# The range check's verdict spread over the last chunk, and the last output tile in two halves

## The chip, the cores and the metric

One core of a Trainium2 chip runs the whole kernel. The metric is the device time of one execution in microseconds, as the median of several runs. Times inside the kernel come from one profiled execution.

## The reference

Attention with a decay bias, then a feed-forward block. For each of 8 batches and 8 heads (576 positions, 64 wide):

```python
cum = np.cumsum(np.maximum(s, 0.0), axis=-1)
bias = -(cum[:, :, :, None] - cum[:, :, None, :])
scores = np.where(causal, -1000000000.0, scale * q @ k.T + np.minimum(bias, 0.0))
attn = softmax(scores)
x = (attn @ v)                      # to [4608 tokens, 512]
xn = x / sqrt(mean(x * x) + 1e-6) * rms_g
out = (silu(xn @ w_gate) * (xn @ w_val)) @ w_out
```

The weights are 512x1536 and 1536x512, the output is 4608x512 in float32.

## The kernel before, in words

The 4608 tokens are worked in 9 chunks of 512 (c = 0 to 8). `ffn(c)` (L658) is the backbone. It has two parts. First come 12 turns (fb = 0 to 11, counted from 0), each with four matmuls for the gate (L668, into a buffer Gp), a tanh on ACT into T (L671), four matmuls for the value (L677, into Vp), and on DVE the product U from T and Gp (L680) and then Ht from U and Vp (L673, the last one L685). I call the products of turn n Un and Hn. Then comes the output projection: four tiles of 128 tokens (tb = 0 to 3), each of 12 matmuls of 512 columns (L690), an eviction on ACT into `osb` (L695) and a store from the SP queue (L697).

All of Gp, Vp and the accumulators Op of the output tiles come from one pool of four PSUM buffers (`psF`, L101). Each allocation takes the buffer of the fourth one before it, so Gp of turn n+2 waits until Un has been computed, and Vp of turn n+2 until Hn has.

The order of instructions on each engine is written out by the program, since the schedule is manual (L771). Between the groups of matmuls `ffn` calls `step()` (L599), which counts a slot and places the work of the attention for later chunks, and one function from each of several side queues if the queue's condition holds: `run_side(dve_side)` (L630) is the one that matters here. In the last two chunks there is no attention work left. Each engine works through its instructions in order.

The fast path holds only while the values stay in a range. For that the kernel collects the largest magnitudes of k and q in `acc` and the sums of squares in `ss_all`, and `decay_range` (L722) adds sums of the decay. `verdict()` (L741) turns these into one flag: four DVE instructions over the statistics ("the sums", L742 to L747, into `stat`), a transpose of `stat` on TensorE (L750), a maximum over it (L752, `mx`), a transpose of `mx` (L754), and a few one-element instructions on DVE with one Exp on ACT (L756 to L768) that end in `flag_i`. It is called once, after `ffn` of chunk 7 and before that of chunk 8 (L912). At the end every engine loads `flag_i` (L927) and branches (L928): in range it skips `general`, which would compute everything again. On SP the load of the flag stands ahead of the last chunk's stores.

Of the kernel before, what the change touches and what calls it, by code (L numbers as in the profile page):

```python
# [12 lines left out]
AF = mybir.ActivationFunctionType  # L13
ALU = mybir.AluOpType
AX = mybir.AxisListType
# [4 lines left out]
DROP_MAX = 576.0 * 2.0 ** -24  # L20
RANGE_MAX = 75.0
SS_MAX = 1.0e37
# [4 lines left out]
def kernel(  # L27
# [12 lines left out]
    nc = tc.nc  # L40
    B, H, S, D = q.shape
    DM = H * D
# [58 lines left out]
    def psF():  # L101
        return pp.tile([128, DM], FP32, name="psF", tag="F", bufs=4)
# [16 lines left out]
    def psT32():  # L119
        return pp.tile([128, 512], FP32, name="psT32", tag="T", bufs=1)  # L120
# [478 lines left out]
    def step(bare=False):  # L599

        slot[0] += 1
        while pending:
            pending.pop(0)()
        moved = False
        if scaled[0] < len(x_list):
            b, qb = x_list[scaled[0]]
            if ready(3, "AV", b, qb, 1):
                x_scale(b, qb)
                scaled[0] += 1
                if not by_pe(b, qb):  # L610
                    assert xt_seq[0] == (b, qb)
                    xt_dma(*xt_seq.pop(0))
                    done["XT", b, qb] = slot[0] + 4
                    moved = True
        run_side(act_side)
        if not moved and x_seq and slot[0] - last["X"] >= 2:
            b, w, c = x_seq[0]
            if (ready(2, "cast", b, 1) and ready(1, "S", b - 2, 4, 0)
                    and (w == 1 or ready(7, "K", b, c))):
                x_seq.pop(0)  # L620
                kq_dma(b, w, c)
                done["X", b, w, c] = last["X"] = slot[0]
                if b >= KB and (w, c) == (0, NSC - 1) and b + 2 < B:
                    casts(b + 2)
        bare = bare or chunk[0] == 0 and 30 <= phase() <= 33
        if slot[0] % 2 and not bare:
            run_side(v_side)
        if not bare:
            run_side(pool_side)
        run_side(dve_side)  # L630
        if can_s():
            pending.append(do_s(s_seq.pop(0)))
            if t_seq and t_seq[0][0] == 1 and can_t():
                do_t(t_seq.pop(0))
            return
        n = 0
        if can_xt():
            do_xt(xt_seq.pop(0))
            n += 1
        if can_av():  # L640
            do_av(av_seq.pop(0))
            n += 1
        if n < 2 and t_seq and can_t():
            do_t(t_seq.pop(0))
# [13 lines left out]
    def ffn(c):  # L658

        x0 = (c * DM) % RING  # L660
        first[0], chunk[0] = slot[0], c
        Ht = mp.tile([128, FB, DM], BF16, name="Ht", tag="Ht", bufs=2)
        pend = None
        for fb in range(FB):
            fs = slice(fb * 128, (fb + 1) * 128)
            Gp = psF()
            for cc in range(CC):
                nc.tensor.matmul(Gp, lhsT=wg_sb[:, cc, fs], rhs=xnT[:, cc, x0:x0 + DM],  # L668
                                 start=(cc == 0), stop=(cc == CC - 1))
            T = mp.tile([128, DM], FP32, name="T", tag="T", bufs=2)  # L670
            nc.scalar.activation(out=T, in_=Gp, func=AF.Tanh, scale=0.5)  # L671
            if pend is not None:
                nc.vector.tensor_tensor(out=Ht[:, fb - 1, :], in0=pend[0], in1=pend[1], op=ALU.mult)  # L673
            step()
            Vp = psF()
            for cc in range(CC):
                nc.tensor.matmul(Vp, lhsT=wv_sb[:, cc, fs], rhs=xnT[:, cc, x0:x0 + DM],  # L677
                                 start=(cc == 0), stop=(cc == CC - 1))
            U = mp.tile([128, DM], BF16, name="U", tag="U", bufs=2)
            nc.vector.scalar_tensor_tensor(out=U, in0=T, scalar=1.0, in1=Gp,  # L680
                                           op0=ALU.add, op1=ALU.mult)
            pend = (U, Vp)
            if fb < FB - 1:
                step()
        nc.vector.tensor_tensor(out=Ht[:, FB - 1, :], in0=pend[0], in1=pend[1], op=ALU.mult)  # L685
        step()
        for tb in range(4):
            Op = psF()
            for fb in range(FB):
                nc.tensor.matmul(Op, lhsT=Ht[:, fb, tb * 128:(tb + 1) * 128],  # L690
                                 rhs=wout_sb[:, fb, :], start=(fb == 0), stop=(fb == FB - 1))
                if fb % 4 == 3 and fb < FB - 1:
                    step()
            osb = mp.tile([128, DM], FP32, name="osb", tag="osb", bufs=3)
            nc.scalar.activation(out=osb, in_=Op, func=AF.Copy, scale=0.5)  # L695
            r0 = c * DM + tb * 128
            nc.sync.dma_start(out=out[r0:r0 + 128, :], in_=osb)  # L697
            step()

    def load_w(src, dst, i):  # L700
# [21 lines left out]
    def decay_range():  # L722

        def row(i):
            e = 255 + 128 * i
            nc.vector.tensor_scalar(out=rng[:, 4 + i:5 + i], in0=cum[:, e:e + 1], scalar1=-1.0,
                                    scalar2=None, op0=ALU.mult)
            nc.scalar.activation(out=s_sb[:, 0:128 * (i + 1)], in_=cum[:, 0:128 * (i + 1)],
                                 func=AF.Exp, bias=rng[:, 4 + i:5 + i],
                                 accum_out=rng[:, 8 + i:9 + i])  # L730

        def over():
            nc.vector.tensor_copy(out=stat[0:BH, 1:2], in_=rng[:, 0:1])
            nc.vector.tensor_tensor(out=rng[:, 11:12], in0=rng[:, 8:9], in1=rng[:, 9:10],
                                    op=ALU.max)
            nc.vector.tensor_tensor(out=stat[0:BH, 2:3], in0=rng[:, 11:12], in1=rng[:, 10:11],
                                    op=ALU.max)
        dve_side.extend((lambda: chunk[0] == B - 1 and slot[0] % 2, f) for f in [
            lambda i=i: row(i) for i in range(3)] + [over])

    def verdict():  # L741
        nc.vector.tensor_reduce(out=stat[:, 0:1], in_=acc, axis=AX.X, op=ALU.max)  # L742
        okc = mp.tile([128, B * NSC], FP32, name="okc")
        nc.vector.tensor_scalar(out=okc, in0=ss_all, scalar1=SS_MAX, scalar2=None, op0=ALU.is_le)
        low = mp.tile([128, 1], FP32, name="low")
        nc.vector.tensor_reduce(out=low, in_=okc, axis=AX.X, op=ALU.min)
        nc.vector.tensor_scalar(out=stat[:, 3:4], in0=low, scalar1=-1.0, scalar2=1.0,  # L747
                                op0=ALU.mult, op1=ALU.add)
        ps = psT32()
        nc.tensor.matmul(ps[0:4, 0:128], lhsT=stat, rhs=ident_f, is_transpose=True)  # L750
        mx = mp.tile([4, 1], FP32, name="mx")
        nc.vector.tensor_reduce(out=mx, in_=ps[0:4, 0:128], axis=AX.X, op=ALU.max)  # L752
        ps2 = psT32()
        nc.tensor.matmul(ps2[0:1, 0:4], lhsT=mx, rhs=ident_f[0:4, 0:4], is_transpose=True)  # L754
        g = mp.tile([1, 8], FP32, name="g")
        nc.vector.tensor_copy(out=g[:, 0:4], in_=ps2[0:1, 0:4])  # L756

        nc.vector.tensor_scalar(out=g[:, 4:5], in0=g[:, 0:1], scalar1=g[:, 0:1], scalar2=8.0625,
                                op0=ALU.mult, op1=ALU.mult)
        nc.scalar.activation(out=g[:, 5:6], in_=g[:, 4:5], func=AF.Exp, scale=2.0)  # L760
        nc.vector.tensor_scalar(out=g[:, 5:6], in0=g[:, 5:6], scalar1=g[:, 2:3], scalar2=DROP_MAX,
                                op0=ALU.mult, op1=ALU.is_le)
        nc.vector.tensor_scalar(out=g[:, 6:7], in0=g[:, 4:5], scalar1=g[:, 1:2],
                                scalar2=RANGE_MAX, op0=ALU.add, op1=ALU.is_le)
        nc.vector.tensor_scalar(out=g[:, 7:8], in0=g[:, 3:4], scalar1=0.5, scalar2=None,
                                op0=ALU.is_le)
        nc.vector.tensor_tensor(out=g[:, 5:6], in0=g[:, 5:6], in1=g[:, 6:7], op=ALU.mult)
        nc.vector.tensor_tensor(out=flag_i, in0=g[:, 5:6], in1=g[:, 7:8], op=ALU.mult)  # L768


    with tc.manual_schedule():  # L771

# [134 lines left out]
        for c in range(NCH):  # L907
            need(c)
            if c == B - 1:
                decay_range()  # L910
            ffn(c)
            if c == B - 1:  # L912
                verdict()
    fast.close()

    general(ctx, tc, q, k, v, out, wg_sb, wv_sb, wout_sb, g_row, cum, ident_bf, flag_i)
# [182 lines left out]
```

## Time and profile before

| | us |
|---|---|
| median of 3 runs (lowest to highest) | 375.38 (375.37 to 375.68) |
| the profiled execution, its own time | 374.85 |
| its span, first to last instruction | 373.2 |
| start of chunk 7, first gate matmul | 304.07 |
| output projection of chunk 7 | 324.79 to 335.31 |
| start of chunk 8, first gate matmul | 336.01 |
| output projection of chunk 8 | 356.73 to 367.25 |
| last eviction | 367.34 to 367.94 |

A line of the timeline shows the start and duration in us, engine, line of the kernel, operation, output and inputs with their shapes, a count where several are merged, and in brackets the idle time of the engine before it and what ended that. PE is TensorE's matmuls, PEld its weight loads. A matmul's duration includes its passage through the array, so the step from one to the next is shorter than its duration. A line of a stretch shows its bounds and length, for each engine the busy time with the number of instructions, then the granted TensorE clock, the share of the DMA engines and GB/s.

### The profile page before, as it was taken

Reading aid. Unit: us, or ns where it says so; the run is one execution under the profiler, and the core shown is the slowest. Engines: PE = TensorE matmul, PEld = TensorE weight load, DVE = VectorE, ACT = ScalarE, POOL = GpSimd, SP = SyncE. Lnnn points to the kernel's source line nnn. Section 1 sums busy time; section 2 is a strip of 40 time slices with the busy share of each in tenths; the row PEclk is TensorE's granted clock in tenths of the full one; section 3 lists DMA queues with packets and bytes.
Section 4 is the critical chain, followed back from the end, with each engine's and each line's share of the span. In section 5 each row is a group of like instructions: output and inputs, shape, how many; then the busy total and the mean of one; then the engine's idle time right before and its main releaser. Section 6 shows DMA issues by size and latency. Waiting matters only on the chain. (4 is left out here: it accounts for less than half of the span.)

```text
span 373.2 us, 6936 instructions
## 1 busy us (share of the span) xinstructions
PE 347.1 (93%) x2356; PEld 161.4 (43%) x2356; DVE 279.6 (75%) x525; ACT 240.0 (64%) x626; POOL 175.2 (47%) x277
## 2 busy tenths in 40 slices
PE   1777899899999999899999999999999999999993
PEld 1443444454444444444444444444444444444441
DVE  6778988589887878788889897795488548837730
ACT  3787787547877597776778776777677644323321
POOL 5866734974846565779856825523322310000000
PEclk9879999999999999999999999999999999999998
DMA  7999999799997599959999997973310230020012
GB/s 228 192 206 262 148 208 210 122 201 222 127 204 104 52 200 161 159 56 204 147 166 223 139 118 151 122 56 44 99 23 14 44 105 3 0 84 31 0 42 78
DMA packets 125626, 46.22 MB, mean 124 GB/s; under 512 B 104912, under 2 KB 120784, under 8 KB 125584
## 3 DMA queue, kind: packets, MB, share of 16 engines
q0 software_dynamic: 59920, 11.80, 43.9%
q1 hardware_dynamic: 53040, 24.33, 34.7%
q10 hardware_dynamic: 12624, 9.59, 10.2%
q8 instruction: 20, 0.33, 0.4%
q14 instruction: 22, 0.18, 0.2%
HBM read 38.16 MB, written 9.44 MB: 128 GB/s over the span
## 5 line engine op out<-in xcount | busy, mean ns | idle before, releaser
L274 ACT ACTIVATE E<-psS,biasK 128x256 bf16<-128x256 f32 (+3 forms) x352 | 115.1, 416 | 19.7 <-PE psS L250 18.0
L668 PE MATMUL psF<-xnT,wg_sb 128*128 128x512 bf16 x432 | 111.1, 379 | 1.9 <-DMA xnT<-xs_sb 0.8
L677 PE MATMUL psF<-xnT,wv_sb 128*128 128x512 bf16 x432 | 111.1, 379 | 0.1
L690 PE MATMUL psF<-wout_sb,Ht 128*128 128x512 bf16 x432 | 102.3, 379 | 0.0
L283 POOL TENSOR_SCALAR_AFFINE_SELECT E<-E 128x512 bf16<-128x512 bf16 x72 | 51.9, 721 | 92.8 <-ACT E L274 92.0
L671 ACT ACTIVATE T<-psF 128x512 f32<-128x512 f32 x108 | 64.4, 598 | 41.5 <-PE psF L668 38.3
L680 DVE SCALAR_TENSOR_TENSOR U<-T,psF 128x512 bf16<-128x512 f32 x108 | 73.6, 682 | 21.8 <-ACT T L671 21.8
L673 DVE TENSOR_TENSOR Ht<-U,psF 128x512 bf16<-128x512 bf16 x99 | 67.7, 684 | 7.5 <-PE psS L250 0.5
L668 PEld LDWEIGHTS <-wg_sb 128*128 128x128 bf16 x432 | 38.7, 98 | 46.3 <-issue 7.5
L677 PEld LDWEIGHTS <-wv_sb 128*128 128x128 bf16 x432 | 38.6, 98 | 42.8 <-issue 4.6
L690 PEld LDWEIGHTS <-Ht 128*128 128x128 bf16 x432 | 38.7, 98 | 42.0 <-issue 2.3
L338 DVE SCALAR_TENSOR_TENSOR xs_sb<-x_sb,al_all,g_row 128x512 bf16<-128x512 bf16 (+1 forms) x40 | 32.4, 810 | 16.6 <-POOL al_all L331 15.0
L695 ACT ACTIVATE osb<-psF 128x512 f32<-128x512 f32 x36 | 21.4, 595 | 33.7 <-PE psF L690 29.3
L321 ACT ACTIVATE xs_sb<-x_sb 128x512 bf16<-128x512 bf16 (+1 forms) x36 | 22.9, 640 | 21.3 <-DVE x_sb L315 21.2
L175 POOL DMA_DIRECT2D v_sb<-in_v_dram x40 | 35.3, 883 | 0.4 <-issue 0.3
L375 DVE TENSOR_TENSOR acc<-acc,mag 128x1280 bf16<-128x1280 bf16 x32 | 29.5, 936 | 0.4
L250 PE MATMUL psS<-kqT 64*128 64x256 bf16 (+2 forms) x304 | 26.6, 260 | 1.4 <-ACT E L274 1.2
L306 PEld LDWEIGHTS <-E 128*128 128x128 bf16 x320 | 22.5, 99 | 12.1 <-POOL E L283 2.2
L328 POOL TENSOR_SCALAR al_all<-ss_all 128x1 f32<-128x1 f32 (+1 forms) x40 | 11.3, 282 | 27.6 <-ACT xs_sb L321 21.5
L300 PEld LDWEIGHTS <-E 128*128 128x128 bf16 x256 | 20.7, 99 | 8.0 <-DVE x_sb L315 0.8
L331 POOL TENSOR_TENSOR al_all<-al_all,mhalf 128x1 f32<-128x1 f32 (+1 forms) x40 | 22.6, 565 | 3.3
L250 PEld LDWEIGHTS <-kqT 64*128 64x128 bf16 x320 | 10.5, 96 | 29.9 <-issue 28.5
(94 smaller groups left out, 279.7 us busy)
## 6 DMA issues: line engine op xcount, KB each, us to landing
out_dram<-osb SPq DMA_DIRECT2D x36, 256.0 KB, 2.3
kq<-in_q_dram ACTq DMA_DIRECT2D x6, 1024.0 KB, 9.5
v_sb<-in_v_dram POOLq DMA_DIRECT2D x32, 128.0 KB, 7.2
kq<-in_k_dram ACTq DMA_DIRECT2D x2, 1024.0 KB, 10.6
kqn<-in_k_dram POOLq DMA_DIRECT2D x16, 128.0 KB, 4.9
wg_sb<-in_moe_w_gate_dram POOLq DMA_DIRECT2D x2, 768.0 KB, 7.3
wv_sb<-in_moe_w_val_dram POOLq DMA_DIRECT2D x2, 768.0 KB, 10.1
wout_sb<-in_moe_w_out_dram POOLq DMA_DIRECT2D x1, 1536.0 KB, 14.1
```

Of the source, the lines that this page charges most:

```text
L175: nc.gpsimd.dma_start(out=v_sb[0:n, b % 2, c, :, 0:64], in_=v[b, :, c * 128:c * 128 + n, :].rearrange("h p d -> p h d"))
L250: nc.tensor.matmul(pair[par][:, j * W:j * W + M], lhsT=kT, rhs=qT, start=(j == 0), stop=(j == nj - 1))
L274: nc.scalar.activation(out=eo, in_=ei, func=AF.Exp, scale=0.125, bias=biasK[:, kb, bh:bh + 1])
L283: nc.gpsimd.affine_select(out=Ev[:, :, 0:nq], in_=Ev[:, :, 0:nq], pattern=[[0, nh], [1, nq]], compare_op=ALU.is_ge, fill=0.0, base=0, chan ...
L338: nc.vector.scalar_tensor_tensor(out=xs_sb[0:n, (b * NSC + qb) % NX, :], in0=x_sb[0:n, (b * NSC + qb) % NX, :], scalar=al_all[0:n, col:col ...
L375: nc.vector.tensor_tensor(out=acc[:, sl], in0=acc[:, sl], in1=mag[:, sl], op=ALU.max)
L668: nc.tensor.matmul(Gp, lhsT=wg_sb[:, cc, fs], rhs=xnT[:, cc, x0:x0 + DM], start=(cc == 0), stop=(cc == CC - 1))
L671: nc.scalar.activation(out=T, in_=Gp, func=AF.Tanh, scale=0.5)
L673: nc.vector.tensor_tensor(out=Ht[:, fb - 1, :], in0=pend[0], in1=pend[1], op=ALU.mult)
L677: nc.tensor.matmul(Vp, lhsT=wv_sb[:, cc, fs], rhs=xnT[:, cc, x0:x0 + DM], start=(cc == 0), stop=(cc == CC - 1))
L680: nc.vector.scalar_tensor_tensor(out=U, in0=T, scalar=1.0, in1=Gp, op0=ALU.add, op1=ALU.mult)
L690: nc.tensor.matmul(Op, lhsT=Ht[:, fb, tb * 128:(tb + 1) * 128], rhs=wout_sb[:, fb, :], start=(fb == 0), stop=(fb == FB - 1))
```

## The change

Two edits. `verdict()` computes nothing itself any more: it makes its tiles and returns four functions, `sums`, `turn`, `row` and `flag`, with the same instructions as before. For chunk 8 (c == B) they are put on the queue `dve_side` before `ffn(8)`, each with the condition that the slot number is a multiple of 3; so `step()` places one in every third slot, one and a half turns apart. By the order of instructions in the changed kernel, the sums stand on DVE between H0 and U1, the maximum of the transposed `stat` between U2 and H2, the copy of the row between H3 and U4, and the flag between U5 and H5. On TensorE the transpose of `stat` stands between the value matmuls of turn 2 and the gate matmuls of turn 3, the transpose of `mx` between the gate and the value matmuls of turn 4; the Exp stands on ACT between the tanh of turns 5 and 6.

The last output tile (chunk 8, tb = 3) is computed in two halves of 256 columns, each with an accumulator of its own, 12 matmuls, an eviction and a store.

```diff
         for tb in range(4):
-            Op = psF()
-            for fb in range(FB):
-                nc.tensor.matmul(Op, lhsT=Ht[:, fb, tb * 128:(tb + 1) * 128],
-                                 rhs=wout_sb[:, fb, :], start=(fb == 0), stop=(fb == FB - 1))
-                if fb % 4 == 3 and fb < FB - 1:
-                    step()
             osb = mp.tile([128, DM], FP32, name="osb", tag="osb", bufs=3)
-            nc.scalar.activation(out=osb, in_=Op, func=AF.Copy, scale=0.5)
             r0 = c * DM + tb * 128
-            nc.sync.dma_start(out=out[r0:r0 + 128, :], in_=osb)
+            halves = 2 if (c, tb) == (NCH - 1, 3) else 1
+            for i in range(halves):
+                Op = psF()
+                cs = slice(i * DM // halves, (i + 1) * DM // halves)
+                for fb in range(FB):
+                    nc.tensor.matmul(Op[:, cs], lhsT=Ht[:, fb, tb * 128:(tb + 1) * 128],
+                                     rhs=wout_sb[:, fb, cs], start=(fb == 0), stop=(fb == FB - 1))
+                    if fb % 4 == 3 and fb < FB - 1:
+                        step()
+                nc.scalar.activation(out=osb[:, cs], in_=Op[:, cs], func=AF.Copy, scale=0.5)
+                nc.sync.dma_start(out=out[r0:r0 + 128, cs], in_=osb[:, cs])
             step()
...
     def verdict():
...
+        def sums():
+            nc.vector.tensor_reduce(out=stat[:, 0:1], in_=acc, axis=AX.X, op=ALU.max)
+            nc.vector.tensor_scalar(out=okc, in0=ss_all, scalar1=SS_MAX, scalar2=None, op0=ALU.is_le)
+            nc.vector.tensor_reduce(out=low, in_=okc, axis=AX.X, op=ALU.min)
+            nc.vector.tensor_scalar(out=stat[:, 3:4], in0=low, scalar1=-1.0, scalar2=1.0,
+                                    op0=ALU.mult, op1=ALU.add)
+
+        def turn():
+            ps = psT32()
+            nc.tensor.matmul(ps[0:4, 0:128], lhsT=stat, rhs=ident_f, is_transpose=True)
+            nc.vector.tensor_reduce(out=mx, in_=ps[0:4, 0:128], axis=AX.X, op=ALU.max)
+
+        def row():
+            ps2 = psT32()
+            nc.tensor.matmul(ps2[0:1, 0:4], lhsT=mx, rhs=ident_f[0:4, 0:4], is_transpose=True)
+            nc.vector.tensor_copy(out=g[:, 0:4], in_=ps2[0:1, 0:4])
+            nc.vector.tensor_scalar(out=g[:, 4:5], in0=g[:, 0:1], scalar1=g[:, 0:1], scalar2=8.0625,
+                                    op0=ALU.mult, op1=ALU.mult)
+
+        def flag():
+            nc.scalar.activation(out=g[:, 5:6], in_=g[:, 4:5], func=AF.Exp, scale=2.0)
...
+        return sums, turn, row, flag
...
             if c == B - 1:
                 decay_range()
+            if c == B:
+                dve_side.extend((lambda: slot[0] % 3 == 0, f) for f in verdict())
             ffn(c)
-            if c == B - 1:
-                verdict()
```

More of the change, by code (lines that the diff above doesn't have):

```diff
@@ L741, in verdict @@
     def verdict():
-        nc.vector.tensor_reduce(out=stat[:, 0:1], in_=acc, axis=AX.X, op=ALU.max)
         okc = mp.tile([128, B * NSC], FP32, name="okc")
-        nc.vector.tensor_scalar(out=okc, in0=ss_all, scalar1=SS_MAX, scalar2=None, op0=ALU.is_le)
         low = mp.tile([128, 1], FP32, name="low")
-        nc.vector.tensor_reduce(out=low, in_=okc, axis=AX.X, op=ALU.min)
-        nc.vector.tensor_scalar(out=stat[:, 3:4], in0=low, scalar1=-1.0, scalar2=1.0,
-                                op0=ALU.mult, op1=ALU.add)
@@ L749, in verdict @@
-        ps = psT32()
-        nc.tensor.matmul(ps[0:4, 0:128], lhsT=stat, rhs=ident_f, is_transpose=True)
         mx = mp.tile([4, 1], FP32, name="mx")
-        nc.vector.tensor_reduce(out=mx, in_=ps[0:4, 0:128], axis=AX.X, op=ALU.max)
-        ps2 = psT32()
-        nc.tensor.matmul(ps2[0:1, 0:4], lhsT=mx, rhs=ident_f[0:4, 0:4], is_transpose=True)
         g = mp.tile([1, 8], FP32, name="g")
-        nc.vector.tensor_copy(out=g[:, 0:4], in_=ps2[0:1, 0:4])
-        nc.vector.tensor_scalar(out=g[:, 4:5], in0=g[:, 0:1], scalar1=g[:, 0:1], scalar2=8.0625,
-                                op0=ALU.mult, op1=ALU.mult)
@@ L760, in verdict @@
[L760 to L766, printed above, removed]
@@ L767, in verdict @@
-        nc.vector.tensor_tensor(out=g[:, 5:6], in0=g[:, 5:6], in1=g[:, 6:7], op=ALU.mult)
-        nc.vector.tensor_tensor(out=flag_i, in0=g[:, 5:6], in1=g[:, 7:8], op=ALU.mult)
+        def sums():
[4 more added lines that the diff above has]
+                                    op0=ALU.mult, op1=ALU.add)
@@ new lines, in flag @@
+        def flag():
+            nc.scalar.activation(out=g[:, 5:6], in_=g[:, 4:5], func=AF.Exp, scale=2.0)
+            nc.vector.tensor_scalar(out=g[:, 5:6], in0=g[:, 5:6], scalar1=g[:, 2:3], scalar2=DROP_MAX,
+                                    op0=ALU.mult, op1=ALU.is_le)
+            nc.vector.tensor_scalar(out=g[:, 6:7], in0=g[:, 4:5], scalar1=g[:, 1:2],
+                                    scalar2=RANGE_MAX, op0=ALU.add, op1=ALU.is_le)
+            nc.vector.tensor_scalar(out=g[:, 7:8], in0=g[:, 3:4], scalar1=0.5, scalar2=None,
+                                    op0=ALU.is_le)
+            nc.vector.tensor_tensor(out=g[:, 5:6], in0=g[:, 5:6], in1=g[:, 6:7], op=ALU.mult)
+            nc.vector.tensor_tensor(out=flag_i, in0=g[:, 5:6], in1=g[:, 7:8], op=ALU.mult)
```

## The prediction

> **What bounds the kernel now.** I read the page first: TensorE is busy for 93% of the span, so time is lost or won where its row of matmuls has a hole, or behind its last matmul.
>
> ```profile
> PE 347.1 (93%) x2356; PEld 161.4 (43%) x2356; DVE 279.6 (75%) x525; ACT 240.0 (64%) x626; POOL 175.2 (47%) x277
> ```
>
> The chain of waits holds only the last eviction here, so I went to the timeline of the last two chunks. First PE (start, duration), where the verdict stands between chunk 7 and chunk 8:
>
> ```profile
> 324.79 10.52 PE L690 MATMUL psF<-wout_sb,Ht 128*128 128x512 bf16 x48
> 335.15 0.27 PE L750 MATMUL psT<-ident_f,stat 128*4 128x128 f32 x1
> 335.80 0.16 PE L754 MATMUL psT<-ident_f,mx 4*1 4x4 f32 x1 [0.37 <-DVE mx L752]
> 336.01 1.02 PE L668 MATMUL psF<-xnT,wg_sb 128*128 128x512 bf16 x4
> ```
>
> 48 matmuls of the output projection follow each other every 0.216 us ((10.52-0.38)/47), so the next one could start at 335.15, which is when L750 starts. The first gate matmul of chunk 8 starts at 336.01. The verdict costs TensorE **0.86 us** here. One chunk earlier, where no verdict stands, there is no hole: 301.48 + 12 x 0.216 = 304.07.
>
> ```profile
> 301.48 2.75 PE L690 MATMUL psF<-wout_sb,Ht 128*128 128x512 bf16 x12
> 304.07 1.03 PE L668 MATMUL psF<-xnT,wg_sb 128*128 128x512 bf16 x4
> ```
>
> Then DVE over the same stretch:
>
> ```profile
> 325.55 0.69 DVE L685 TENSOR_TENSOR Ht<-U,psF 128x512 bf16<-128x512 bf16 x1
> 326.16 2.81 DVE L742 TENSOR_REDUCE stat<-acc 128x1 f32<-128x2560 bf16 x1
> ...
> 329.32 0.15 DVE L747 TENSOR_SCALAR stat<-low 128x1 f32<-128x1 f32 x1
> ...
> 337.70 0.69 DVE L680 SCALAR_TENSOR_TENSOR U<-T,psF 128x512 bf16<-128x512 f32 x1 [0.36 <-ACT T L671]
> 338.49 0.69 DVE L673 TENSOR_TENSOR Ht<-U,psF 128x512 bf16<-128x512 bf16 x1
> 339.43 0.69 DVE L680 SCALAR_TENSOR_TENSOR U<-T,psF 128x512 bf16<-128x512 f32 x1 [0.25 <-ACT T L671]
> ```
>
> Two things are to be seen. The long part of the verdict, 326.16 to 329.47, runs under the output projection of chunk 7, in which DVE has nothing else to do: it is free. And inside chunk 8 DVE rests only 0.25 us in each turn of 1.73 us (337.70 to 339.43).
>
> **The change, part by part.**
>
> *The hole goes: -0.86 us.* With no verdict between the chunks the gate matmul starts at 335.15. Call this t0; what follows is counted from it, with the offsets that chunk 8 shows now from its own start at 336.01.
>
> *The sums move under the gate/value loop: +1.97 us.* By the order of instructions in the changed kernel the four sums stand on DVE behind U0, H0 and ahead of U1. U0 starts at t0+1.69 (337.70), H0 at +2.48 (338.49); the reduce follows a product by 0.61 (325.55 to 326.16), so +3.09; from it to L747 are 3.16 (326.16 to 329.32), +6.25; then U1 at about +6.40, ending at +7.09. Now it starts at +3.42. Who waits: psF has four buffers and each turn takes two, so the gate matmul of turn 3 (turns counted from 0, as fb) takes the buffer that U1 frees. PE would be there at +5.18 (three turns of 1.73). A DVE result reaches PE after 0.06 (mx ends at 335.74, L754 starts at 335.80), so this matmul starts at +7.15: PE stands still for 1.97 us. The margin was 1.0 us (U ends at +2.38 of its own turn, the buffer is wanted at +3.45), and the block brings 3.31. The transpose of stat stands ahead of this same matmul and waits for stat until about +6.46; with its 0.27 it is through before +7.15 and costs nothing of its own.
>
> *What is late next.* H1 ends at +7.88, and the value matmul of turn 3 wants its buffer at 7.15+0.86 = +8.01: no wait. U2 ends at +8.49, wanted at +8.88. The reduce of mx (0.28), the copy and scaling of the row (0.35) and the flag (0.69 from 336.65 to 337.34) stand one and a half turns apart; DVE gains 0.25 in each turn and has the margin of 1.0, so I cost them at nothing. If that cover failed, they would cost at most their sum, 1.3 us. On ACT the Exp (0.20) goes between two tanh, in front of each of which ACT idles 1.13; the value that it waits for is ready a turn earlier. SP and POOL read the flag ahead of their branch, SP also ahead of the last stores: now at 337.4, then at about t0+14, and the first store behind it is wanted at t0+24. Nobody waits.
>
> *The transpose of mx: +0.21 us.* It stands in PE's row between a gate and a value group. L754 to the next matmul are 0.21 now (335.80 to 336.01). The other end is 0.03, the step between the small 128x65 matmuls. I take 0.21: it is the same instruction.
>
> *The last tile by halves: -0.30 us.* 24 matmuls of 256 columns for 12 of 512. Matmuls of 128 columns in the same array shape, L184, follow each other every 0.05 us, each with its own weight load, so loads don't bind and 24 x 0.108 is what 12 x 0.216 was: no change on PE. The first half is evicted and issued while PE still computes the second (SP's issue takes 0.33), so it holds up nothing. What ends last is the second half. A 128x256 copy on ACT takes 0.378 where the full eviction takes 0.597 (min/median/max in ns):
>
> ```profile
> L207 ACT ACTIVATE kqT<-psT x3: 377/378/395, 49.5 to 128.9; 128x256 bf16<-128x256 bf16 x3
> L695 ACT ACTIVATE osb<-psF x4: 597/597/598, 359.5 to 367.3; 128x512 f32<-128x512 f32 x4
> ```
>
> That is 0.22 at best. The last store lands 2.8 us after its issue, the three before it 2.0 to 2.2. In its window stand two transfers of instructions on the same engines, the first at 368.3, ahead of the store's own data; then one engine trails until 370.3.
>
> ```profile
> q8 instruction: 1, 0.02, 1.8%
> q14 instruction: 1, 0.01, 0.6%
> issues: line engine op xcount, KB each, median us to landing
> out_dram<-osb SPq DMA_DIRECT2D x1, 256.0 KB, 2.8
> ```
>
> These come with the branch behind PE's last matmul and don't move, so most of the 0.22 is hidden behind that engine. A 2 KB packet of a store takes some 86 ns (28.8% of 16 engines over 2.4 us, 128 packets), a 1 KB packet of the first loads 73 ns, among other traffic. Eight per engine: 0.10 by the loads, 0.34 by half of the store's own. The bounds of the whole tail are 0.10 and 0.22+0.34 = 0.56; I take 0.30, as the store's own row is the nearer one. [...]
>
> **Sum:** -0.86 + 1.97 + 0.21 - 0.30 = **+1.02 us**. The profiled execution took 374.85 us (span 373.2), so 375.87. It lies 0.53 below the median of the runs shown, 375.38; put on that, the forecast is **376.4 us**, 0.27% slower.
>
> **The rivals.**
>
> *The end is worth more (not slower).* If the halved store no longer meets the instruction transfers, it lands as the others do, 0.8 earlier, and the eviction counts in full: 0.8+0.22+0.1 for 0.30, sum +0.2, 375.6. It decides from the point where the store's data are through before 368.3. For it: the first half is gone by then. Against it: the second is issued only at about 0.5 behind PE's end, the transfer comes 1.0 behind it, and data follow an issue by 0.7.
>
> *No stall (faster).* The change does what it says only if the wait on U1 is slack that the timeline doesn't show. Then the hole is gone, 0.86, the tail 0.30, less 0.21: -0.95, 374.4. It holds if the sums took less than 1.3 us; L742 alone takes 2.81, and nothing in the new place makes it shorter.
>
> *The clock falls (slower still).* Granted clock is the column before the DMA share:
>
> ```profile
> 14.00:16.00 2.00, 1.14 (x12) 0.76 (x12) 1.68 (x4) 1.95 (x6) 1.95 (x3) 0.94 2.10 168
> 16.00:18.00 2.00, 1.48 (x17) 0.81 (x16) 1.53 (x4) 0.52 (x2) 1.74 (x3) 0.50 1.16 209
> ...
> 30.00:32.00 2.00, 0.68 (x6) 0.38 (x6) 2.00 (x2) 0.93 (x2) 2.00 (x3) 1.00 1.09 350
> ```
>
> It fell to 0.50 from 16 to 22 us (with 0.94 before and 0.85 behind, 6.8 us of half clock), after gaps of 0.4 to 0.8 us among short matmuls, but not after 30 to 32, where PE was busy for 0.68 of 2.00. A stall of 1.97 lies nearer to the second. If it falls as long, 6.8 us at half clock cost 3.4: 379.8. [...]
>
> *Weight loads bind the halves (slower).* At 0.216 for each of 24 the tile takes 2.6 more: 379.0. The step of L184 speaks against it.
>
> **How the numbers follow.** Forecast 0.75, more from the end 0.10, no stall 0.07, clock 0.05, weight loads 0.03. The forecast's own bounds: stall 1.85 to 2.05, transpose 0.03 to 0.21, tail 0.56 to 0.10, so +0.5 to +1.3: 375.8 to 376.7. The range takes in the first rival and some of the uncosted insertions: 375.3 to 377.0; outside it are the last three, 0.15. About 0.2%, 0.75 us, is what a measurement of this kernel can tell from no change, and the forecast lies near that line: 0.53 of its 0.75 fall above it, 0.20 within, 0.02 below. So slower 0.53+0.05+0.03 = 0.61, same 0.20+0.10 = 0.30, faster 0.02+0.07 = 0.09.
>
> **What would show it.** After: the gate matmul of chunk 8 right behind the last L690; in turn 2 to 3 PE idle for about 2 us, first on stat, then on U; DVE without idle time from H0 to U5; 0.2 at the transpose of mx; the last eviction near 0.38 and a landing of about 2.5. I am wrong if PE's idle time in chunk 8 is well under 1.9 us, if it comes back at a later turn, or if the end behind the last matmul shrinks by more than 0.6.

## The result, and the profile after

| | before | after |
|---|---|---|
| median of 8 runs each, us | 375.42 | 377.11 |
| lowest of the runs | 374.67 | 376.21 |
| the profiled execution | 374.85 | 377.02 |
| its span | 373.2 | 375.3 |

The ratio is 1.0044 (95% interval 1.0030 to 1.0059): the change makes the kernel 1.7 us slower by the medians (1.1 to 2.2 by the interval). The forecast was 1.02 us slower, 376.4, in a range that ended at 377.0, so the direction was right and the size was not. The profiled executions differ by 2.17 us, a little more than the medians.

TensorE in the profile after, from the end of chunk 7 (start, duration; brackets: idle before and what ended it):

```profile
324.65 10.52 PE L695 MATMUL psF<-wout_sb,Ht 128*128 128x512 bf16 x48
335.01 1.03 PE L668 MATMUL psF<-xnT,wg_sb 128*128 128x512 bf16 x4
...
339.32 1.03 PE L677 MATMUL psF<-xnT,wv_sb 128*128 128x512 bf16 x4
341.56 0.27 PE L759 MATMUL psT<-ident_f,stat 128*4 128x128 f32 x1 [1.21 <-DVE stat L754]
342.07 1.02 PE L668 MATMUL psF<-xnT,wg_sb 128*128 128x512 bf16 x4 [0.23 <-DVE U L680]
...
344.75 0.16 PE L764 MATMUL psT<-ident_f,mx 4*1 4x4 f32 x1
344.84 1.04 PE L677 MATMUL psF<-xnT,wv_sb 128*128 128x512 bf16 x4
```

The hole between the chunks is gone: 324.65 + 48 x 0.216 is 335.01, and there the gate matmul starts. But the gate matmul of turn 3, which three turns of 1.73 would put at 340.19, starts at 342.07. DVE shows why:

```profile
337.49 0.69 DVE L673 TENSOR_TENSOR Ht<-U,psF 128x512 bf16<-128x512 bf16 x1
338.10 2.81 DVE L751 TENSOR_REDUCE stat<-acc 128x1 f32<-128x2560 bf16 x1
...
341.27 0.15 DVE L754 TENSOR_SCALAR stat<-low 128x1 f32<-128x1 f32 x1
341.34 0.68 DVE L680 SCALAR_TENSOR_TENSOR U<-T,psF 128x512 bf16<-128x512 f32 x1
342.12 0.69 DVE L673 TENSOR_TENSOR Ht<-U,psF 128x512 bf16<-128x512 bf16 x1
```

The sums push U1 to 341.34, and TensorE goes on 0.05 after U1's end. The waits of TensorE over the rest of the chunk are these two, and no others:

```profile
PE psT L759 <- DVE stat L754: 1.2, 1, 1.2
PE psF L668 <- DVE U L680: 0.2, 1, 0.2
```

From the start of chunk 7's projection to that of chunk 8's are 33.15 us, where they were 31.94: TensorE loses 1.21. The rest of the loss lies behind its last matmul. The last tile's evictions and stores, of the profile after (durations in ns: shortest, median, longest; then the stores' time in us from issue to landing):

```profile
L699 ACT ACTIVATE osb<-psF x2: 384/384/384, 367.1 to 368.4; 128x256 f32<-128x256 f32 x2
...
DMA to landing us min/median/max: 1.7/2.6/3.4
```

The first half lands after 1.7 us, the last one only after 3.4. And behind SP's branch (the second of its two, behind the waits for the stores) come SP's closing instructions (L1094 before, L1104 after); DRAIN is the name of some of them. Before:

```profile
L928 SPq COMPARE_BRANCH  x2: 38/50/61, 368.3 to 371.0; - x2
L1094 SPq DRAIN  x3: 7/7/13, 372.3 to 372.6; - x3
```

After:

```profile
L938 SPq COMPARE_BRANCH  x2: 38/50/61, 369.2 to 372.4; - x2
L1104 SPq DRAIN  x3: 7/13/127, 373.6 to 375.0; - x3
```

The last of three drains comes 1.6 us behind SP's branch before (371.0 to 372.6) and 2.6 after (372.4 to 375.0), and takes 127 ns for 7. To the end of the span the branch has 2.17 us before and 2.98 after. The other engines end only behind this drain: after, their own last drains start at 374.0 to 374.3, and the last instruction of each comes at 375.2 to 375.3, behind SP's at 375.0.

### The profile page after: what moved, and what is told of

Same layout as the page of the kernel before. It is cut to its first block, busy times and chain, and to the rows that moved or that the text cites. A ratio compares the mean times of both kernels' runs of the same rounds, so it can differ in the third digit from the quotient of the medians.

```text
span 375.3 us, 6963 instructions
## 1 busy us (share of the span) xinstructions
PE 347.3 (93%) x2368; PEld 162.4 (43%) x2368; DVE 278.5 (74%) x525; ACT 240.3 (64%) x627; POOL 175.6 (47%) x277
## 4 chain that ended last, share of the span: by engine, by line
PE 65%; DVE 11%; POOL 10%; issue 6%; ACT 4%; DMA 3%; ACTq 0%; POOLq 0%; DVEq 0%
PE psF L695 20%; PE psF L668 18%; PE psF L677 18%; PE psS L250 4%; POOL v_sb L175 2%; ACT E L274 2%; POOL al_all L331 2%; DVE U L680 2%; POOL E L283 2%; DVE Ht L673 2%; POOL kqn L141 1%; DMA kq<-in_k_dram 1%; DVE x_sb L315 1%; DVE xs_sb L338 1%; DVE acc L375 1%
## 5 line engine op out<-in xcount | busy, mean ns | idle before, releaser
L695 PE MATMUL psF<-wout_sb,Ht 128*128 128x512 bf16 (+1 forms) x444 | 102.3, 374 | 0.0
L695 PEld LDWEIGHTS <-Ht 128*128 128x128 bf16 x444 | 39.9, 98 | 41.1 <-issue 2.3
L699 ACT ACTIVATE osb<-psF 128x512 f32<-128x512 f32 (+1 forms) x37 | 21.6, 584 | 33.2 <-PE psF L695 30.8
```

The lines of the kernel that those rows point to most:

```text
L695: nc.tensor.matmul(Op[:, cs], lhsT=Ht[:, fb, tb * 128:(tb + 1) * 128], rhs=wout_sb[:, fb, cs], start=(fb == 0), stop=(fb == FB - 1))
```

## The experiments

Three theories stood at the start. **A:** the sums hold TensorE back, and the halves are harmless or a small gain. **B:** a part of the loss comes from the halves. **C**, added after the first four runs: the halves cost time through the number of SP's instructions, not through the store. In the table, the second column is SP's instructions up to its branch, counted in the trace; the third runs from the end of the last output matmul to SP's branch, the fourth from there to the end of the span, both in us of one profiled execution. Each ratio is to the kernel before, timed beside that run. The edits shown are against the changed kernel; those of "One DMA more on SP", "Two instructions more on SP" and the two single runs with an engine late are against the kernel before.

| kernel | SP instr. | to SP's branch | to the end | ratio to before, 95% interval |
|---|---|---|---|---|
| before | 272 | 3.76 | 2.17 | 1 |
| after | 274 | 4.00 | 2.98 | 1.0044 (1.0030 to 1.0059) |
| verdict only | 272 | 3.77 | 2.17 | 1.0037 (1.0014 to 1.0059) |
| halves only | 274 | 4.26 | 3.15 | 1.0014 (0.9985 to 1.0042) |
| sums early | 272 | 4.00 | 2.17 | 0.9988 (0.9964 to 1.0012) |
| sums early, halves | 274 | 3.66 | 2.89 | 0.9989 (0.9961 to 1.0018) |
| one DMA more on SP | 272 | 4.09 | 2.17 | 1.0006 (0.9987 to 1.0026) |
| halves, SP count kept | 272 | 3.98 | 2.17 | 0.9995 (0.9981 to 1.0008) |
| ACT late | 272 | 3.76 | 2.57 | 1.0006 (0.9992 to 1.0020) |
| sums early, ACT late | 272 | 4.45 | 2.63 | 0.9974 (0.9957 to 0.9990) |
| two instructions more on SP | 274 | 4.05 | 3.04 | 1.0029 (1.0006 to 1.0052) |
| sums early, halves, SP count kept | 272 | 4.03 | 2.17 | 0.9964 (0.9950 to 0.9978) |
| TensorE late | 272 | 3.27 | 2.62 | 0.9999 (0.9982 to 1.0016) |
| sums early, TensorE late | 272 | 3.26 | 2.65 | 0.9975 (0.9947 to 1.0003) |

**Verdict only.**

```diff
-            halves = 2 if (c, tb) == (NCH - 1, 3) else 1
+            halves = 1
```

> The verdict in four steps within the last chunk, the last tile in one piece as before. Theory A (the sums on DVE hold TensorE back, and the halves are harmless or a small gain): TensorE stands for 1.9 us ahead of turn 3 as in the changed kernel, its last matmul comes 1.1 us later than before, and the time is 1.0 to 1.3 us above before, or as long as the changed kernel if the halves do nothing. Theory B (a part of the loss comes from the halves, whose last store lands 3.4 us after its issue against 2.8): the same 1.1 us on TensorE, but the end behind the last matmul as long as before, so 0.5 us or more below the changed kernel.

Measured: the gate matmul of turn 3 waits 1.22 for stat and 0.23 for U, and from projection to projection are 33.15 us, to a hundredth what the changed kernel shows. The end is that of before. The time is 1.4 us above before (0.5 to 2.2). The stall is the verdict's, and by the timed runs it accounts for most of the loss (0.0037 of 0.0044); the intervals of this run and of the changed kernel overlap, so the timed runs alone don't show that the halves cost something on top. By the profiles of before and after the two parts are nearly equal: 1.21 us on TensorE and 1.05 behind its last matmul.

**Halves only.**

```diff
             if c == B - 1:
                 decay_range()
-            if c == B:
-                dve_side.extend((lambda: slot[0] % 3 == 0, f) for f in verdict())
             ffn(c)
+            if c == B - 1:
+                for f in verdict():
+                    f()
```

> The last tile in two halves, the verdict whole between the last two chunks as before. Theory A: 0 to 0.3 us faster than before, the last eviction 0.38 for 0.60 us, and a landing of about 2.5 us. Theory B: 0.4 to 0.8 us slower than before, with a landing above 3 us because the store waits behind the transfer of instructions on one engine.

Measured: 0.5 us above before, with an interval from 0.6 below to 1.6 above, so unclear in time. The profile is clear: the landing, 3.7 us, is above 3 as theory B has it, and 0.98 more pass from SP's branch to the end. The transfer of 16 KB of instructions starts 2.0 us behind the last matmul here, where it is 1.1 in the kernels before and after.

**Sums early.** The sums stay under the projection of chunk 7, the rest goes into chunk 8, the last tile stays whole.

```diff
-            halves = 2 if (c, tb) == (NCH - 1, 3) else 1
+            halves = 1
...
-            if c == B:
-                dve_side.extend((lambda: slot[0] % 3 == 0, f) for f in verdict())
             ffn(c)
+            if c == B - 1:
+                sums, *rest = verdict()
+                sums()
+                dve_side.extend((lambda: slot[0] % 3 == 0, f) for f in rest)
```

> The four sums on DVE right behind chunk 7, under its output projection, as before; the other three steps of the verdict within chunk 8; the last tile in one piece. Theory A: no stall in chunk 8, the hole of 0.86 us between the chunks gone, 0.2 to 0.3 us for each of the two transposes in TensorE's row, so the last matmul 0.3 to 0.5 us earlier and the time 0.3 to 0.5 us below before. A rival that puts the stall down to the other steps (the waits of the transposes, the Exp on ACT) expects the time above before.

TensorE in chunk 8 of this run:

```profile
337.89 1.03 PE L668 MATMUL psF<-xnT,wg_sb 128*128 128x512 bf16 x4
338.75 0.27 PE L759 MATMUL psT<-ident_f,stat 128*4 128x128 f32 x1
338.86 1.03 PE L677 MATMUL psF<-xnT,wv_sb 128*128 128x512 bf16 x4
...
341.55 0.16 PE L764 MATMUL psT<-ident_f,mx 4*1 4x4 f32 x1
341.64 1.04 PE L668 MATMUL psF<-xnT,wg_sb 128*128 128x512 bf16 x4
```

No brackets: the profile names no wait here. The transpose of stat costs 0.11 (338.75 to 338.86), that of mx 0.19 (the step from the matmul before, due at 341.45, to 341.64). Projection to projection is 31.39 us, 0.55 less than before, which is 0.86 less these two. So the stall comes from the sums alone. The ratio of the timed runs, 0.9988, agrees in size but its interval reaches above 1.

**Sums early and halves.** The verdict as in that run, the last tile in halves.

> As the run with the sums early, and the last tile in two halves. Theory A: 0 to 0.3 us below that run, the fastest of the four. Theory B: 0.4 to 0.8 us above it.

Measured: 0.9989, no better and no worse than without the halves, so neither theory's time; 2.89 from SP's branch to the end.

**One DMA more on SP.** Every kernel with halves so far had the long closing, none without. But they also have one store more on SP. So, in the kernel before:

```diff
-        nc.sync.dma_start(out=g_row, in_=moe_rms_g.rearrange("(o d) -> o d", o=1).to_broadcast([128, DM]))
+        for i in (0, 1):
+            cs = slice(i * DM // 2, (i + 1) * DM // 2)
+            nc.sync.dma_start(out=g_row[:, cs], in_=moe_rms_g[cs].rearrange("(o d) -> o d", o=1).to_broadcast([128, DM // 2]))
```

> The kernel before, but the load of g_row, early in the SP queue, in two column halves: one SP instruction more, nothing else changed. Theory C (behind the last branch SP's closing instructions are brought in by a transfer of 16 KB, and one instruction more in SP's program puts one of them behind that transfer): from SP's branch to the end of the span 2.9 to 3.2 us as in the kernels with halves, not 2.2 as before, and the time 0.7 to 0.9 us above before. A rival by which it is the halved store itself that lengthens the end: 2.2, and the time of before.

Measured: 2.17 and the time of before, which spoke against theory C. But the trace shows why it was no test of it: SP issues one DMA more and waits once less, so it still has 272 instructions. So it decides nothing.

**Halves with SP's count kept.** The verdict stands whole between the chunks, as in "Halves only"; the other edit is:

```diff
-                nc.sync.dma_start(out=out[r0:r0 + 128, cs], in_=osb[:, cs])
+                eng = nc.scalar if (c, tb) == (NCH - 1, 0) else nc.sync
+                eng.dma_start(out=out[r0:r0 + 128, cs], in_=osb[:, cs])
```

> Only the halves, but the store of the tile three before the last is issued by ACT, so that SP has as many instructions as before. Theory C: from SP's branch to the end 2.2 us again; the landing as long as with halves, so within 0.3 us of before. The rival: 2.9 to 3.2 as with the halves alone, and 0.4 to 0.8 us above before.

Measured: 2.17 again with the halved store in place, and 0.2 us below before (0.7 below to 0.3 above). The halved store as such does not lengthen the closing.

**ACT late, alone and with the sums early.** These two, and the later two with TensorE late, ask whose transfer of instructions the last store meets.

```diff
+        for i in range(3):
+            junk = mp.tile([128, DM], FP32, name="T", tag="T", bufs=2)
+            nc.scalar.activation(out=junk, in_=wout_sb[:, i, :], func=AF.Copy)
     fast.close()
```

> The kernel before, with three copies of 128x512 on ACT behind the last eviction, whose result nobody reads, so that ACT comes to its branch 1.8 us later. If the transfer of instructions that holds up the last store (it starts 0.3 us behind ACT's branch) is ACT's, it moves to about 370.2, the store lands in 2.0 instead of 2.8 us, SP's branch comes 0.7 to 0.8 us earlier, and so does the end. If it is TensorE's or SP's, it stays 1.1 us behind the last matmul, and the time stays or grows by up to 0.5 us.

> The sums early, the other steps within chunk 8, the last tile whole, and the same three copies on ACT. 0.55 us less on TensorE as in the run with the sums early, and 0.7 to 0.8 us less at the end if the transfer is ACT's: 1.2 to 1.4 us below before. Only 0.5 below before if it is not.

Measured: ACT branches at 370.3 in the first, yet the transfer of 16 KB starts at 369.1, 1.1 us behind the last matmul as before. It is not ACT's. The time stays, at 1.0006. With the sums early the ratio is 0.9974, 1.0 us (0.4 to 1.6) below before, between the two forecasts. Its stretch from projection to projection is 31.39 us, as without the copies, and its end is longer. The transfer starts 1.8 us behind the last matmul there, but 0.5 ahead of ACT's branch: not ACT's either.

**Two instructions more on SP**, whole last tile, whole verdict:

```diff
-            nc.sync.dma_start(out=out[r0:r0 + 128, :], in_=osb)
+            parts = 2 if c == NCH - 1 and tb < 2 else 1
+            for i in range(parts):
+                cs = slice(i * DM // parts, (i + 1) * DM // parts)
+                nc.sync.dma_start(out=out[r0:r0 + 128, cs], in_=osb[:, cs])
```

> The kernel before with the verdict whole and the last tile whole, but the stores of the first two tiles of the last chunk, which nobody waits for, each issued in two column halves from SP. With their waits SP has two instructions more, as many as in the changed kernel (the run with g_row in halves had one DMA more but one wait less, so as many as before, and could not tell). Theory C: from SP's branch to the end 2.9 to 3.2 us, not 2.17, and a time 0.7 to 0.9 us above before. The rival, that the halved last store lengthens the end: 2.17, and the time of before within 0.3 us.

SP's drains in this run:

```profile
L1097 SPq DRAIN  x3: 7/13/127, 372.6 to 374.1; - x3
```

The drain of 127 ns is there again, 1.36 us behind the one before it, without any halved last store; the time is 1.1 us above before (0.2 to 2.0). Theory C holds: four of four kernels with 274 instructions on SP have this drain of 127 ns, and none of the ten with 272 (127 or 128 ns against 7).

**Sums early, halves, SP's count kept.**

> Sums early, the other steps within chunk 8, halves, and the store of the tile three before the last issued by ACT, so that SP has as many instructions as before. Theory C: from SP's branch to the end 2.17 us, 0.7 to 0.9 us below the run with the sums early and halves; about 0.5 us below before in all, as the halves themselves bring 0 to 0.2.

```profile
L1107 SPq DRAIN  x3: 7/7/13, 372.2 to 372.6; - x3
```

Measured: 2.17 from SP's branch to the end, and 0.9964 (0.9950 to 0.9978), 1.35 us below before. It beats both kernels, and its interval lies wholly below that of the changed kernel. The gain is larger than the 0.5 us forecast, and the profile doesn't explain it: from the start of chunk 7's projection to the end of the span are 48.14 us, where before has 48.40.

**TensorE late, alone and with the sums early.**

```diff
             ffn(c)
+            if c == B:
+                warm(4)
```

> The kernel before with four matmuls more on TensorE behind the last one, whose result nobody reads: TensorE comes to its branch 0.86 us later. If the 16 KB transfer that holds up the last store is TensorE's, it starts 1.1 us behind the last of these, at about 2.0 us behind the last matmul of the output, when most of the store's data are through; the store lands 2.0 to 2.4 instead of 2.8 to 3.4 us after its issue. The end gains 0.3 to 0.8 us from that, unless TensorE's own closing, also 0.86 us later, takes its place: then 0 to 0.2. If the transfer is SP's, nothing moves.

> Sums early, the other steps within chunk 8, the last tile whole, and the same four matmuls behind the last one. 0.55 us less on TensorE, plus what the run with the four matmuls alone gains: 0.5 to 1.3 us below before.

The four matmuls and the stores of the last chunk, of the first of the two:

```profile
369.22 1.03 PE L597 MATMUL psF<-wg_sb,ident_bf 128*128 128x512 bf16 x4
```

```profile
DMA to landing us min/median/max: 2.0/2.1/2.3
```

The transfer of 16 KB starts at 371.9, 2.6 us behind the last output matmul, and the last store lands after 2.3 us instead of 2.8. It moved by 1.4 us for TensorE's 0.86, more than expected, and the same in the second run. That it is TensorE's shows more plainly in TensorE's own branches (PEldq; the longest is the last one) in before, after and this run:

```profile
L928 PEldq COMPARE_BRANCH  x2: 83/1728/3373, 364.1 to 367.4; - x2
L938 PEldq COMPARE_BRANCH  x2: 83/1978/3873, 366.8 to 368.5; - x2
L930 PEldq COMPARE_BRANCH  x2: 83/1976/3870, 366.8 to 370.4; - x2
```

The last branch takes 3.3 to 4.1 us in the fourteen kernels, and in each it ends 1.3 to 1.5 us behind the end of the transfer. The transfer starts 0.9 us behind the branch's start in ten of them, 1.5 in the two with TensorE late, 1.6 with sums early and ACT late, 1.8 with the halves only; why it is later in these is open.

With TensorE late its closing is late too: its drain starts at 374.4, behind SP's second at 374.0, where before it came 1.5 us ahead of it (370.9 and 372.4). From SP's branch to the end are 2.62 us for 2.17, and the time is that of before: the gain is given back at once. In the second run the time is 0.9 us below before (2.0 below to 0.1 above), as in the other runs with the sums early.

## Why the prediction missed, point by point

*The hole goes, -0.86:* right. The gate matmul follows the projection at 335.01 with nothing between them.

*The sums hold TensorE back, +1.97:* right in mechanism and nearly in size. Measured +1.88 (342.07 for 340.19), first on stat, then on U, as stated. The difference is U1, which follows the sums by 0.07 and not by 0.15. Nothing else in the chunk waited, so the insertions costed at nothing cost nothing, and DVE rests again from U7 on (0.18 ahead of it, 0.24 ahead of U8).

*The transpose of mx, +0.21:* measured 0.19. *TensorE in sum:* +1.32 forecast, +1.21 measured.

*The last tile by halves, -0.30:* this is the step that failed, in two places: it took the end of the instruction transfer as fixed ("don't move"), and it put the extra store on SP at nothing ("it holds up nothing"). From the end of the last matmul to the end of the span the profiled execution grew from 5.93 to 6.98 us, so +1.05. Three terms make it up.

- The issue of the last store comes 0.26 earlier (0.71 to 0.45 behind the last matmul), for 0.22 at best in the forecast.
- The landing takes 0.50 longer (3.05 to 3.55 from issue to SP's branch), where 0.1 to 0.34 less was forecast. The prediction had seen the transfer of instructions in the store's window and taken it to be tied to TensorE's branch; the tie is borne out by the runs with ACT late (1.1 us behind the last matmul, as before) and TensorE late (2.6). The prediction counted eight packets at half price behind it, and they came out: from the end of the transfer to SP's branch are 1.71 us before and 1.27 after, 0.44 less (1.60 to 1.76 with whole and 1.26 to 1.32 with halved last tiles, wherever TensorE is not late). What failed is the fixed end: the transfer started 1.1 us behind the last matmul in both, but took 1.60 us where it had taken 0.93, so it ended 0.68 later. 120 of the 128 packets were through by 370.14; the last eight came behind the transfer, from 371.06 to 371.72, at 0.05 to 0.15 each. The store's window after (q8 is the queue of this transfer):

```profile
q8 instruction: 1, 0.02, 2.5%
q14 instruction: 1, 0.01, 0.5%
out_dram<-osb SPq DMA_DIRECT2D x1, 128.0 KB, 3.4
```

  The first half, which meets no transfer, lands after 1.7 us where a whole tile takes 2.0, so 0.3 less for 128 KB; by these two the part that doesn't shrink with the size is 1.4 us, an estimate.

  The transfer took 0.93 to 1.31 us with whole and 1.00 to 1.65 with halved last tiles, TensorE not late. Whether the halves lengthen it, one profile of each kernel doesn't show: this cause stays open. From the last matmul to SP's branch are 3.76 to 4.09 with whole and 3.66 to 4.26 with halved last tiles, in the kernels where no engine is late: the halves neither gain nor lose there that these profiles could tell.
- The closing behind SP's branch takes 0.81 longer (2.17 to 2.98). No step of the prediction counted this. "It holds up nothing" was said of the extra store by its time on SP, 0.33; what it adds is two instructions (the store and a wait) ahead of SP's last ones.

In timed runs the sign is the same and the size smaller: with the halves 0.0014, 0.0001 and 0.0007 more in the ratio than without (halves only against before; sums early; verdict), each with an uncertainty of some 0.003 to 0.004 to each side, so none is clear by itself. With SP's count kept, the halves come out at 0.0005 (against before) and 0.0024 (against sums early) less, as unclear. By the pair that differs least, for the closing alone, two instructions more on SP against before, it is 0.0029, 1.1 us.

*The rivals.* The end was not worth more but less, so that the first rival fails: eight packets still come behind the transfer. Its condition, the other data through before the transfer starts, isn't enough either: with the halves only 120 packets were through by 369.57 and the transfer started at 369.78, yet the last eight came at 370.76 and the store landed after 3.7 us. The stall came, so "no stall" fails. The clock stayed at 1.00 through it (the column before the DMA share and GB/s):

```profile
340.00:342.00 2.00, 0.62 (x3) 0.13 (x2) 1.93 (x5) 0.12 (x1) 0.00 (x0) 1.00 0.00 0
342.00:344.00 2.00, 1.93 (x9) 0.87 (x9) 1.90 (x5) 0.60 (x1) 0.00 (x0) 1.00 0.03 8
```

Weight loads didn't bind the halves: 60 matmuls of the last projection, 24 of them short, take 10.55 where 48 took 10.52. The terms on TensorE lay within their bounds. The range missed by 0.1 us because the tail's bounds, a gain of 0.10 to 0.56, left out any loss. That it came so near is partly luck: the range reached 0.3 us past these bounds to make room for insertions that then cost nothing.

## What to carry to other kernels

Work that is free where its engine rests isn't free where the engine is paced: here the sums, 3.24 us on DVE, brought U1 2.91 us later (to 341.34; 3.42 behind the chunk's first gate matmul, as before, is 338.43), and TensorE lost 1.88 of it. So look for the idle time of the engine at the new place, not for the hole at the old one, and split off only the small part that made the hole. An instruction added to a queue is not only its own time: here SP had two more, one of them a store of 0.33 us, and the closing behind its branch took 2.98 us for 2.17. So a tail should be costed with bounds on both sides and its last lines compared kernel by kernel.

## What the runs showed of the hardware

Two instructions more on SP ahead of its branch came with 0.7 to 1.0 us more in the closing (2.89 to 3.15 us for 2.17). In the four kernels that show it, a transfer of 16 KB of instructions (16384 bytes in the trace) starts 0.5 to 0.8 us behind SP's branch, and the late drain comes 0.7 to 1.2 us behind its end. Where SP has 272 instructions there is such a transfer too, but the drain doesn't come so far behind it: 0.14 us in before (transfer from 371.54 to 372.47, drain at 372.61), and ahead of its end in the fastest kernel (drain at 372.55, transfer until 372.97). Why two instructions more make the drain later was not shown; that the closing instructions are brought in by this transfer, as theory C has it, is the author's reading.

The other transfer of 16 KB, the one tied to TensorE's last branch, falls among the last store's packets, of which some come last, one behind the other: after, the transfer ran from 369.49 to 371.09, and eight of 128 packets came from 371.06 to 371.72; before, the transfer ran from 368.37 to 369.31, the last five 2 KB packets of the store followed each other from 369.92 to 370.32, when all others were through by 369.92, and it landed after 2.8 us instead of 2.0. That the eight are the share of one DMA engine, as the prediction has it, is an estimate from the count (128 packets on the 16 engines of the page); the trace doesn't name a packet's engine.
